# Sums of x blocks made two pairs ahead on buffers of their own, and squares of rows behind the copies of sums, in an attention and token-mixing kernel

## The chip, the cores and the metric

The kernel runs on one core of a Trainium2 chip. The metric is the time of one execution in microseconds (us) on the device; the figure before is the median of three runs. Five engines work side by side: TensorE (PE; its weight loads are PEld), VectorE (DVE), ScalarE (ACT), GpSimd (POOL) and SyncE (SP), which here only issues DMAs. POOL and ACT issue DMAs too.

## The reference

```python
x = A_x                                             # (1, 2048, 640) float32
g = sigmoid((x * gate_w).sum(-1, keepdims=True))
qkv = x @ wqkv                                      # 32 heads of 20
p = softmax(q @ k.T * 20 ** -0.5)                   # for each head
a = (p @ v) @ wo
h = layernorm(x)                                    # over the 640 channels
u = gelu(einsum("bsd,sf->bdf", h, w1) + b1)         # mixing over the 2048 tokens
b = einsum("bdf,fs->bds", u, w2) + b2
out = g * a + (1 - g) * b.transpose
```

Everything is float32.

## The kernel before

A product in full precision is made of three matmuls: each operand is split into a high part (rounded copy, on ScalarE) and a low part (the rest, a subtraction on VectorE), and the products high-high, high-low and low-high are summed in PSUM. `hi_lo` is this split.

The stages in order of time are: the products of x with the first two groups of columns of q and of k (`qk_unit(m, w, q)`: 128 columns m by 512 rows q, m below 5 for q, from 5 on for k); the product for v together with the sums for the gate and for the mean of each row; the rest of q and k, with the normalized rows h; the two products of the token mixing with the first scores beside them; attention; and the last product with wo.

Each `qk_unit` puts 15 matmuls into a PSUM bank, copies it out as a high part `evh` (ScalarE) and a low part `evl` (VectorE, a ring of two buffers) and stores both, to q_d or k_d. For the first three column groups of k (c = 0, 1, 2) it also forms the difference of two neighbouring 512-row blocks: `kf` keeps a copy of an even unit, the odd unit subtracts, splits the difference into `dh` and `kf` and stores four tiles to kd_d. For c = 1 (unit m = 6) kf and dh lie in the ring k8 (three buffers), and the four stores are issued by POOL.

The product for v is a fast 2 by 2 block scheme with seven products, for each pair of 128-row blocks of x. Eight pairs, `i` = 0 to 7, each with:

- `v_load(i)`: a DMA on SP brings the pair's block of x transposed, `vx`. `v_sums(i)`: POOL makes four sums of its quarters, T1 to T4, in `vr`. `v_split(i)`: `hi_lo` of vr into `vT`, in the ring k8. vx, vr and the rows `xn` lie in the ring q4, of six buffers.
- `split_wv` splits the eight combinations of v's weights (A11, A12, A22, S1 to S4, and number 7) among the eight qk units n = 0 to 7 ahead of this stage.
- `v_head(i)`: products X (A11) and Y (A12), 15 matmuls; the first copy of X's sum into `sn` on ScalarE (`v_snap`); the split of the next pair; an output tile.
- `v_body(i)`: X goes on with T2 S2 (6 matmuls), second copy of X; Z with T1 S1 (9); X goes on with T3 S3 (6), third copy of X; an output tile. T3's products add to the bank that the second copy reads.
- `v_tail(i)`, which runs after the head of pair i + 1: X with T4 A22, Z with S4, 18 matmuls, two output tiles, then `negm`, the negative mean of the rows, on VectorE, and `stats_unit` for both row blocks: the sum of squares of (x − mean) on ScalarE, from rows `xn` that POOL's DMA loads.

An output tile `vt` (a ring of three) gets its constant columns by memsets on POOL, its data from ScalarE (L536, where no sum is added) or VectorE (L538), and is stored to v_d by SP.

In this part the order of TensorE, ScalarE and VectorE is that of the program text (`manual_schedule`); the order of POOL and SP is chosen by the scheduler from its own estimate of times. Every queue works in order. A tile of a ring waits until the former tile in its buffer is no longer used. `xr` is a ring of two 640-column buffers, for weights of q and k before the split.

Of the kernel before, what the change touches and what calls it, by code (L numbers as in the profile page):

```python
# [7 lines left out]
F32 = mybir.dt.float32  # L8
F32R = mybir.dt.float32r
# [4 lines left out]
P = 128  # L14
S, D, H, DH, F = 2048, 640, 32, 20, 1728
NP = H // 2
NT = S // P
NC = D // P
# [13 lines left out]
def gated_mix(ctx, tc, xT, x, wqk, wv0, wv1, wo, w1, w1t, b1, w2, b2, out):  # L32
    nc = tc.nc
# [17 lines left out]
    def mm3(ps, pairs, between=lambda i: None):  # L51
        n = len(pairs)
        for i, (ah, al, bh, bl) in enumerate(pairs):
            for k, (a, b) in enumerate(((ah, bh), (ah, bl), (al, bh))):
                nc.tensor.matmul(ps, a, b, start=(i == 0 and k == 0), stop=(i == n - 1 and k == 2))  # L55
            between(i)
# [28 lines left out]
    def one_tile(shape, name):  # L85
        n = one_count[0] % 4
        one_count[0] += 1
        return psum.tile(shape, F32, tag=("s3", "pv", "one0", "one1")[n], bufs=1, name=name)
# [9 lines left out]
    def k8(shape, dt, name):  # L98
        return base.tile(shape, dt, tag="k8", bufs=3, name=name)

    def q4(shape, dt, name):
        return base.tile(shape, dt, tag="q4", bufs=6, name=name)
# [189 lines left out]
    p1 = p1s.enter_context(tc.tile_pool(name="p1", bufs=1, side="right"))  # L292
# [5 lines left out]
    def w_dma(m, eng=nc.scalar):  # L298
        raw = p1.tile([P, NC, P], F32, tag="xr", bufs=2, name=f"wr{m}")
        eng.dma_start(raw, wqk[m])  # L300
        return raw
# [9 lines left out]
    k_first = {}  # L311

    def qk_unit(m, w, q):
        wh, wl = w
        ps = one_tile([P, 512], f"qk{m}_{q}")
        mm3(ps, [(wh[:, c], wl[:, c], xh[c][q], xl[c][q]) for c in range(NC)], *([keep_warm] if m == q == 0 else []))
        hi = p1.tile([P, 512], F32R, tag="evh", bufs=3, name=f"evh{m}_{q}")
        tag, bufs = ("kf", 1) if (m, q) == (2 * NC - 1, 3) else ("evl", 2)
        lo = p1.tile([P, 512], F32R, tag=tag, bufs=bufs, name=f"evl{m}_{q}")
        hi_lo(hi, lo, ps, hi_eng=nc.scalar)  # L320
        c = m - NC
        dst = q_d if m < NC else k_d
        rows = slice((m % NC) * P, (m % NC + 1) * P)
        cols = slice(q * 512, (q + 1) * 512)
        stores = [(dst[i, rows, cols], t.bitcast(F32)) for i, t in enumerate((hi, lo))]
        if (m, q) == (2 * NC - 1, 3):
            return stores
        for a in stores:
            nc.sync.dma_start(*a)
        if not 0 <= c * P < DROWS:  # L330
            return
        if q % 2 == 0:
            if q == 0 or c == 2:
                k_first[c] = p1.tile([P, 512], F32, tag="kf", bufs=1, name=f"kf{c}_{q}")
            elif c:
                k_first[c] = k8([P, 512], F32, f"kf{c}_{q}")
            else:
                k_first[c] = px.tile([P, 512], F32, tag="kf2", bufs=1, name=f"kf{c}_{q}")
            nc.vector.tensor_copy(k_first[c], ps)
            return  # L340
        put = nc.gpsimd.dma_start if c < 2 else nc.sync.dma_start
        put(kd_d[0, rows, cols], hi.bitcast(F32))
        put(kd_d[1, rows, cols], lo.bitcast(F32))
        kd = k_first.pop(c)
        nc.vector.tensor_sub(kd, kd, ps)
        if c == 2:
            dh = p1.tile([P, 512], F32R, tag="evh", bufs=3, name=f"dh{c}_{q}")
        elif c:
            dh = k8([P, 512], F32R, f"dh{c}_{q}")
        else:  # L350
            dh = px.tile([P, 512], F32R, tag="dh", bufs=1, name=f"dh{c}_{q}")
        hi_lo(dh, kd.bitcast(F32R), kd, hi_eng=nc.scalar)
        cols = slice((q - 1) * 512, q * 512)
        put(kd_d[0, rows, cols], dh.bitcast(F32))
        put(kd_d[1, rows, cols], kd)
# [33 lines left out]
    xr = {(c, 0): x_dma(c, 0) for c in range(NC)}  # L389
    raws = {NC: w_dma(NC, nc.sync)}  # L390
# [27 lines left out]
    A11, A12, A22, S1, S2, S3, S4 = range(7)  # L418
# [4 lines left out]
    r11, r21, r22 = (wr[0][:, 2 * i: 2 * i + 2] for i in range(3))  # L423
    r12, rc = wr[1][:, :2], wr[1][:, 2:5]
# [6 lines left out]
    def split_wv(i, raw):  # L431
        hi_lo(wvh[i], wvl[i], raw, hi_eng=nc.scalar)
# [7 lines left out]
    def v_load(i):  # L440
        v_xs[i] = q4([P, 4, 2 * P], F32, f"vx{i}")
        nc.sync.dma_start(v_xs[i], xT[:4 * P, 2 * P * i: 2 * P * (i + 1)].rearrange("(c p) s -> p c s", p=P))

    def v_sums(i):
        r = v_xs.pop(i)
        r11, r12, r21, r22 = (r[:, 2 * k: 2 * k + 2, n * P:(n + 1) * P] for k in range(2) for n in range(2))
        v_rs[i] = q4([P, 8, P], F32, f"vr{i}")
        t = [v_rs[i][:, 2 * j: 2 * j + 2] for j in range(4)]
        nc.gpsimd.tensor_sub(t[T1], r12, r11)
        nc.gpsimd.tensor_sub(t[T2], r22, t[T1])  # L450
        nc.gpsimd.tensor_sub(t[T3], r22, r12)
        nc.gpsimd.tensor_sub(t[T4], r21, t[T2])

    def v_split(i):
        t = v_ts[i] = k8([P, 2, 8, P], F32R, f"vT{i}")
        hi_lo(t[:, 0], t[:, 1], v_rs.pop(i), hi_eng=nc.scalar)

    for n in range(8):
        if n == 1:
            split_wv(A11, r11)  # L460
            split_wv(A12, r12)
        if n == 2:
            split_wv(A22, r22)
            nc.vector.tensor_add(r22, r22, r21)
            nc.vector.tensor_sub(r21, r11, r21)
            v_load(0)
        if n == 3:
            split_wv(S1, r22)
            nc.vector.tensor_sub(r22, r22, r11)
            v_sums(0)  # L470
        if n == 4:
            nc.vector.tensor_sub(rc[:, 2:], rc[:, :1], rc[:, 1:2])
            split_wv(7, rc)
            v_load(1)
        if n == 5:
            split_wv(S2, r22)
            nc.vector.tensor_sub(r12, r12, r22)
        if n == 6:
            split_wv(S3, r21)
        if n == 7:  # L480
            split_wv(S4, r12)
        qk_unit((1, NC + 1)[n // 4], w[(1, NC + 1)[n // 4]], n % 4)
        if n == 0:
            w[NC + 1] = load_w(NC + 1, raws[NC + 1])
    v_split(0)
    nc.gpsimd.dma_start(b1_t, b1)
    nc.gpsimd.dma_start(b2_t, b2)
    xjs = {}

    def stats_load(t):  # L490
        if t < NT:
            xjs[t] = q4([P, D], F32, f"xn{t}")
            nc.gpsimd.dma_start(xjs[t], x[t * P:(t + 1) * P, :])

    def stats_unit(t):
# [13 lines left out]
    def v_w(i, k):  # L509
        return wvh[i][:, k], wvl[i][:, k]  # L510
# [34 lines left out]
    def v_head(i):  # L545
        t0 = 2 * i
        v_ps[i] = [v_bank(i, k) for k in range(3)]
        X, Y, Z = v_ps[i]
        v_mm(X, [(v_x(t0, k), v_w(A11, k)) for k in range(2)], True)
        v_mm(Y, [(v_x(t0, 2 + k), v_w(A12, k)) for k in range(2)] + [(v_x(t0, 4), v_w(7, 0))], True)  # L550
        a = v_snap(i, 0)
        if i + 1 < NT // 2:
            v_split(i + 1)
        v_out(0, t0, Y, a)

# [11 lines left out]
    def v_tail(i):  # L567
        t0, t1 = 2 * i, 2 * i + 1
        X, Y, Z = v_ps.pop(i)
        v_mm(X, [(v_t(i, T4, k), v_w(A22, k)) for k in range(2)] + [(v_x(t0, 4), v_w(7, 1))], False)  # L570
        v_mm(Z, [(v_x(t1, 2 + k), v_w(S4, k)) for k in range(2)] + [(v_x(t1, 4), v_w(7, 2))], False)
        v_ts.pop(i)
        v_out(1, t0, X)
        v_out(0, t1, Z, v_sn.pop(i))
        c = slice(t0, t0 + 2)
        nc.vector.tensor_scalar_mul(negm[:, c], gs[:, c, 1], -1.0 / D)
        for t in (t0, t1):
            stats_unit(t)

    for i in range(NT // 2):  # L580
        if i + 1 < NT // 2:
            v_sums(i + 1)
        if i + 2 < NT // 2:
            v_load(i + 2)
        v_head(i)
        if i:
            v_tail(i - 1)
        for t in (2 * i, 2 * i + 1):
            stats_load(t)
        v_body(i)  # L590
        if i == NT // 2 - 3:
            raws[2] = w_dma(2)
        if i == NT // 2 - 1:
            w[2] = load_w(2, raws[2])
    qk_unit(2, w[2], 0)
    v_tail(NT // 2 - 1)
    nc.scalar.activation(rstd, ssq, AF.Sqrt, bias=eps_t, scale=1.0 / D)
    nc.vector.reciprocal(rstd, rstd)
    nc.scalar.activation(g_t, gs[:, :, 0], AF.Exp, scale=-1.0)
# [340 lines left out]
    for n, _ in enumerate(steps):  # L940
# [5 lines left out]
        while done + 2 <= S_AHEAD and dve_work(done) < dve_room(n):  # L946
            if done == 48:
                s_src[1] = base_stack(1, False, None)
            if done == 4 * 128 + 40:
                held, drip[:] = list(drip), []  # L950
                st_src[0] = base_stack(0, True, None)
                put = lambda *a: drip.append(lambda: nc.sync.dma_start(*a))
# [253 lines left out]
    for p in range(NP):  # L1206
# [3 lines left out]
        for it in range(32):  # L1210
# [10 lines left out]
            if it == 14 and due_stack:  # L1221
                n = due_stack.pop()
                if n < NP:
                    s_src[n] = s_stack(n)
            if p == NP - 1:
# [4 lines left out]
                if it in (5, 20, 25):  # L1230
                    q = (5, 20, 25).index(it)
# [78 lines left out]
    for t in range(2, NT):  # L1310
        q = {4: 4, 7: 5, 10: 6, 12: 7}.get(t)
# [67 lines left out]
```

## Time and profile before

| | |
|---|---|
| median of three runs | 1792.18 us (1789.33 to 1794.43) |
| profiled execution | 1789.76 us |
| its span, from the first to the last record | 1787.9 us |
| mean granted TensorE clock | 0.994 |
| busy: PE | 1760.3 us (98%) |
| ACT | 1488.6 us (83%) |
| DVE | 1252.4 us (70%) |
| POOL | 690.7 us (39%) |

The profile comes from one execution. A row of a timeline gives the start in us from the span's start, the length, engine, line, operation, the tile written and those read, and in brackets how long the engine had been idle before and what released it. L502 is the matmul of the values' product, L525 the copy sn, L41 and L44 the high and low part of a split, L497 the squares, L342, L343, L354 and L355 the stores to kd_d. A list of waits gives the total, the number and the longest. "issue" is time in which an engine waited for nothing that the profile shows.

### The profile page before, as it was taken

The numbers are of one execution on the slowest core, as the hardware profiler recorded it, in microseconds if no ns is written. First come the engines' busy times: TensorE is split into PE (matmuls) and PEld (weight loads), VectorE is DVE, ScalarE is ACT, GpSimd is POOL, SyncE is SP. The second block draws the span as 40 slices with busy tenths as digits, with TensorE's granted clock in tenths as the row PEclk, the third lists the DMA queues.
The fourth block names the chain that finished last, engine by engine and source line by source line (L and its number), as shares of the span: only waits on it lengthen the run. The fifth ranks groups of instructions, "written<-read, shape, count | busy, mean of one in ns | idle before, by whom it ended". The sixth has DMA issues, their size and how long they took to land.

```text
span 1787.9 us, 39575 instructions
## 1 busy us (share of the span) xinstructions
PE 1760.3 (98%) x14972; PEld 1088.5 (61%) x14972; DVE 1252.4 (70%) x2443; ACT 1488.6 (83%) x2547; POOL 690.7 (39%) x1025
## 2 busy tenths in 40 slices
PE   9789999999999999999999999999999999999999
PEld 7688899999999999733333333333333333333379
DVE  5532369989899988877676767676777667677336
ACT  4344368888888888699999999999999999999951
POOL 1451658789878777412111211111231212111320
PEclk9899999999999999999999999999999999999999
DMA  9764986566677555336304314234173143311345
GB/s 329 225 206 155 293 241 171 153 177 184 184 190 184 152 154 157 99 74 141 73 19 95 65 32 92 50 70 103 35 144 76 26 102 76 79 20 43 125 158 181
DMA packets 160433, 229.39 MB, mean 128 GB/s; under 512 B 66684, under 2 KB 97292, under 8 KB 156816
## 3 DMA queue, kind: packets, MB, share of 16 engines
q1 hardware_dynamic: 141454, 197.01, 40.3%
q0 software_dynamic: 15568, 23.95, 5.6%
q10 hardware_dynamic: 3220, 5.90, 1.2%
q8 instruction: 118, 1.93, 0.5%
q14 instruction: 73, 0.60, 0.1%
HBM read 171.07 MB, written 55.36 MB: 127 GB/s over the span
## 4 chain that ended last, share of the span: by engine, by line
PE 93%; issue 2%; DMA 2%; ACT 1%; DVE 1%; POOL 1%; SPq 0%; DVEq 0%; ACTq 0%; POOLq 0%
PE pv L1058 28%; PE st L1157 22%; PE s L213 12%; PE y L49 10%; PE u L49 9%; PE qk L55 5%; PE v L502 2%; PE a L1277 1%; PE a_one L1277 1%; PE a_pv L1277 1%; PE a_s L1277 1%; ACT xn L497 0%; DMA v_d<-vt 0%; DMA kd_d<-dh 0%; DMA k_d<-evl 0%
## 5 line engine op out<-in xcount | busy, mean ns | idle before, releaser
L219 DVE TENSOR_REDUCE mx<-s 128x1 f32<-128x512 f32 x1280 | 834.7, 686 | 282.8 <-PE s L213 155.8
L1175 ACT ACTIVATE p<-st 128x512 f32<-128x512 f32 x1022 | 560.9, 614 | 0.0
L1058 PE MATMUL pv<-p,v 128*32 128x512 f32 x4088 | 544.5, 605 | 0.0
L1164 ACT ACTIVATE p<-st 128x1024 f32<-128x1024 f32 x511 | 529.8, 1037 | 1.2 <-PE st L1157 1.1
L1157 PEld LDWEIGHTS st<-qs_True,ks_True 62*128 62x128 f32 x2044 | 243.9, 185 | 432.6 <-ACT p L1164 426.8
L1157 PE MATMUL st<-qs_True,ks_True 62*128 62x512 f32 x2044 | 494.1, 445 | 0.0
L213 PE MATMUL s<-ks_False,qs_False 60*128 60x512 f32 x1152 | 323.2, 391 | 0.4 <-ACT p L1175 0.2
L44 POOL TENSOR_TENSOR wl<-wr,wh 128x512 fp32r<-128x512 f32 x228 | 275.3, 1218 | 61.4 <-ACT wh L41 46.7
L238 DVE CUSTOM_DVE_ANT_0 ov<-s,ov 128x512 f32<-128x512 f32 x384 | 263.7, 687 | 35.8 <-PE s L213 24.9
L213 PE MATMUL s<-sk,sq 60*128 60x512 f32 x896 | 281.3, 394 | 0.0
L228 ACT ACTIVATE ov<-s 128x512 f32<-128x512 f32 x384 | 228.4, 597 | 61.4 <-PE s L213 54.1
L1039 POOL DMA_DIRECT2D l_d<-oev x124 | 60.5, 494 | 382.1 <-DVE oev L1031 378.3
L49 PE MATMUL y<-gh,wh 64*128 64x320 f32 x896 | 198.0, 305 | 0.0
L213 PEld LDWEIGHTS s<-ks_False,qs_False 60*128 60x128 f32 x1152 | 194.2, 184 | 3.1 <-ACT p L1175 0.7
L1058 PEld LDWEIGHTS pv<-p,v 128*32 128x32 f32 x4088 | 80.5, 108 | 187.0 <-issue 175.3
L49 PE MATMUL y<-gh,wl 64*128 64x320 f32 x832 | 191.4, 305 | 0.0
L49 PE MATMUL y<-gl,wh 64*128 64x320 f32 x832 | 191.4, 305 | 0.0
L49 PE MATMUL u<-hh,wh 64*128 64x320 f32 x864 | 191.3, 304 | 0.0
L49 PE MATMUL u<-hl,wh 64*128 64x320 f32 x864 | 191.2, 304 | 0.0
L41 ACT ACTIVATE wh<-wr 128x512 fp32r<-128x512 f32 (+3 forms) x247 | 146.8, 598 | 41.6 <-PE y L49 15.6
L49 PE MATMUL u<-hh,wl 64*128 64x320 f32 x800 | 179.6, 304 | 0.0
L213 PEld LDWEIGHTS s<-sk,sq 60*128 60x128 f32 x896 | 166.2, 186 | 15.0
(217 smaller groups left out, 2478.0 us busy)
## 6 DMA issues: line engine op xcount, KB each, us to landing
wr<-in_w_dram SPq DMA_DIRECT2D x192, 256.0 KB
ks_True<-k_d SPq DMA_DIRECT2D x96, 160.0 KB
qs_True<-q_d SPq DMA_DIRECT2D x192, 80.0 KB
qs_False<-q_d SPq DMA_DIRECT2D x96, 80.0 KB
v_d<-vt SPq DMA_DIRECT2D x32, 212.0 KB
sk<-k_d SPq DMA_DIRECT2D x42, 160.0 KB
sq<-q_d SPq DMA_DIRECT2D x84, 80.0 KB
v<-v_d SPq DMA_DIRECT2D x15, 424.0 KB
```

Source lines behind the costliest of these rows:

```text
L41: nc.scalar.activation(hi, src, AF.Copy)
L44: (lo_eng or nc.vector).tensor_sub(lo, src, hi.bitcast(F32))
L49: nc.tensor.matmul(ps[k], a[r], b[r], start=start, stop=stop)
L55: nc.tensor.matmul(ps, a, b, start=(i == 0 and k == 0), stop=(i == n - 1 and k == 2))
L213: nc.tensor.matmul(ps, qs[half][r, t * P:(t + 1) * P], ks[r, kc * 512:(kc + 1) * 512], start=True, stop=True)
L219: nc.vector.tensor_reduce(mx[:, slot, j, t: t + 1], ps, axis=AX.X, op=OP.max)
L228: nc.scalar.activation(over[j, kc], ps, AF.Relu)
L238: nc.vector.tensor_tensor_reduce(ov, ps, ov, 1.0, -3.0e38, OP.add, OP.max, mx[:, slot, j, t: t + 1])
L1058: nc.tensor.matmul(pv[r: r + 32, :], v_tiles[p][:, kt, VW * j: VW * j + 32], pt[j, c], start=(kt == 0), stop=(kt == NT - 1))
L1157: nc.tensor.matmul(ps, ks[r, kt * P:(kt + 1) * P], qs[qh][r, c * 512:(c + 1) * 512], start=True, stop=True)
L1164: nc.scalar.activation(pt, ps, AF.Exp, scale=SCALE)
L1175: nc.scalar.activation(pt, ps, AF.Exp, scale=SCALE)
```

## The change

The sums of a block are made two pairs ahead of their use and the loads three ahead, and the split of the second pair is made before the loop. The rows xn leave q4 for the ring xr; kf and dh of c = 1 leave k8 for xr, and their stores to kd_d go from POOL's queue to SP's. The splits of v's weights move to earlier units. The squares of a pair stand behind the third copy of the next pair's body, and the rows of the next squares are loaded after them. The weights of the next q unit (m = 2) are loaded into q4 and split one pair earlier.

```diff
             elif c:
-                k_first[c] = k8([P, 512], F32, f"kf{c}_{q}")
+                k_first[c] = p1.tile([P, 512], F32, tag="xr", bufs=2, name=f"kf{c}_{q}")
...
-        put = nc.gpsimd.dma_start if c < 2 else nc.sync.dma_start
+        put = nc.gpsimd.dma_start if c < 1 else nc.sync.dma_start
...
         elif c:
-            dh = k8([P, 512], F32R, f"dh{c}_{q}")
+            dh = p1.tile([P, 512], F32R, tag="xr", bufs=2, name=f"dh{c}_{q}")
...
         if n == 1:
             split_wv(A11, r11)
             split_wv(A12, r12)
+            v_load(0)
         if n == 2:
             split_wv(A22, r22)
             nc.vector.tensor_add(r22, r22, r21)
             nc.vector.tensor_sub(r21, r11, r21)
-            v_load(0)
+            v_sums(0)
         if n == 3:
             split_wv(S1, r22)
             nc.vector.tensor_sub(r22, r22, r11)
-            v_sums(0)
-        if n == 4:
             nc.vector.tensor_sub(rc[:, 2:], rc[:, :1], rc[:, 1:2])
             split_wv(7, rc)
+        if n == 4:
+            split_wv(S2, r22)
+            nc.vector.tensor_sub(r12, r12, r22)
             v_load(1)
         if n == 5:
-            split_wv(S2, r22)
-            nc.vector.tensor_sub(r12, r12, r22)
+            split_wv(S3, r21)
+            split_wv(S4, r12)
+            v_sums(1)
         if n == 6:
-            split_wv(S3, r21)
-        if n == 7:
-            split_wv(S4, r12)
+            v_split(0)
+            v_load(2)
         qk_unit((1, NC + 1)[n // 4], w[(1, NC + 1)[n // 4]], n % 4)
...
-    v_split(0)
+    v_split(1)
...
     def stats_load(t):
         if t < NT:
-            xjs[t] = q4([P, D], F32, f"xn{t}")
+            xjs[t] = p1.tile([P, D], F32, tag="xr", bufs=2, name=f"xn{t}")
...
-        if i + 1 < NT // 2:
+        if 1 < i + 1 < NT // 2:
             v_split(i + 1)
...
         nc.vector.tensor_scalar_mul(negm[:, c], gs[:, c, 1], -1.0 / D)
-        for t in (t0, t1):
+    def v_stats(i):
+        for t in (2 * i, 2 * i + 1):
             stats_unit(t)
 
+    for i in range(2):
+        stats_load(i)
     for i in range(NT // 2):
-        if i + 1 < NT // 2:
-            v_sums(i + 1)
         if i + 2 < NT // 2:
-            v_load(i + 2)
+            v_sums(i + 2)
+        if i + 3 < NT // 2:
+            v_load(i + 3)
         v_head(i)
         if i:
             v_tail(i - 1)
-        for t in (2 * i, 2 * i + 1):
-            stats_load(t)
         v_body(i)
-        if i == NT // 2 - 3:
-            raws[2] = w_dma(2)
-        if i == NT // 2 - 1:
+        if i:
+            v_stats(i - 1)
+            for t in (2 * i, 2 * i + 1):
+                stats_load(t)
+        if i == NT // 2 - 4:
+            raws[2] = q4([P, NC, P], F32, "wr2")
+            nc.scalar.dma_start(raws[2], wqk[2])
+        if i == NT // 2 - 2:
             w[2] = load_w(2, raws[2])
     qk_unit(2, w[2], 0)
     v_tail(NT // 2 - 1)
+    v_stats(NT // 2 - 1)
```

## The prediction

> **What bounds the kernel now.** I read the page first, then the table of windows by stage, the list of waits of TensorE, the timelines of TensorE, ScalarE and VectorE around the waits, and the list of DMA issues.
>
> The table of windows, whose columns are stretch and length, then busy time and count of PE, PEld, DVE, ACT, POOL, then granted clock, DMA share and GB/s:
>
> ```profile
> 62.50:161.60 99.10, 77.09 (x450) 72.46 (x449) 33.63 (x89) 38.08 (x84) 38.30 (x137) 0.90 0.58 190
> 161.60:1787.90 1626.30, 1622.18 (x14270) 966.83 (x14268) 1179.71 (x2298) 1422.35 (x2415) 635.86 (x853) 1.00 0.45 118
> ```
>
> TensorE is the bound. From 161.6 us to the end it idles 4.1 of 1626 us, at the full clock. Ahead of that lies the stage of the values' product, which the change rewrites: 77.1 of 99.1 us busy, at a mean clock of 0.90. Since TensorE has no slack behind it, what this stage gains or loses moves the end by as much. Who holds TensorE there, in the list of waits (total, times, longest):
>
> ```profile
> PE v L502 <- ACT sn L525: 20.1, 9, 9.4
> PE qk L55 <- ACT wh L41: 1.2, 1, 1.2
> PE v L502 <- DVE vT L44: 0.5, 1, 0.5
> ```
>
> ScalarE's copy of a sum (sn) ends nine of the waits. In TensorE's timeline (start, length, ... , idle before and who ended it) the first three of the nine:
>
> ```profile
> 74.93 0.64 PE L502 MATMUL v<-wvh,vT 128*128 128x322 f32 x1 [9.39 <-ACT sn L525]
> ...
> 81.53 0.42 PE L502 MATMUL v<-wvh,vT 128*128 128x322 f32 x1 [2.00 <-ACT sn L525]
> ...
> 92.15 0.42 PE L502 MATMUL v<-wvh,vT 128*128 128x322 f32 x1 [0.80 <-ACT sn L525]
> ```
>
> The 9.39 and the 2.00 us stand before the first and the second pair of rows; the other seven (20.1 − 9.4 − 2.0 = 8.7 us) come once in each pair from the second on, like the 0.80 us at 92.15, always in front of the third product T3 with S3.
>
> **What stands before sn.** ScalarE's timeline, at the start and in one steady pair:
>
> ```profile
> 72.97 0.63 ACT L41 ACTIVATE dh<-kf 128x512 fp32r<-128x512 f32 x1 [6.25 <-DVE kf L345]
> 73.51 1.04 ACT L41 ACTIVATE vT<-vr 128x1024 fp32r<-128x1024 f32 x1
> 74.46 0.42 ACT L525 ACTIVATE sn<-v 128x322 f32<-128x322 f32 x1
> 80.09 1.06 ACT L41 ACTIVATE vT<-vr 128x1024 fp32r<-128x1024 f32 x1 [5.21 <-DMA kd_d<-dh]
> ...
> 99.98 0.81 ACT L497 ACTIVATE xn<-xn,negm 128x640 f32<-128x640 f32 x1
> 100.70 0.19 ACT L497 ACTIVATION_READ_ACCUMULATOR xn<-xn,negm 128x1 f32 x1
> 100.79 0.42 ACT L525 ACTIVATE sn<-v 128x322 f32<-128x322 f32 x1
> ```
>
> There are three causes, one for each part of the change. The first sn (74.46) is queued behind the last dh, which waited for VectorE. The second sn runs right after the split vT at 80.09, which waited 5.2 us for a store of dh: vT takes its buffer from the ring k8, where dh and kf lay. In the steady pairs two squares (L497) are in front of sn.
>
> **The steps and their cost.** No instruction is added or removed; order, buffers and queues change. For the floor I need the pace of the matmuls:
>
> ```profile
> 86.20:91.10 4.90, 4.90 (x35) 4.89 (x33) 2.52 (x8) 1.57 (x5) 3.04 (x7) 1.00 0.24 88
> 74.90:92.10 17.20, 13.94 (x69) 13.02 (x69) 6.21 (x16) 5.77 (x12) 6.69 (x16) 0.79 0.59 177
> 92.10:151.15 59.05, 51.12 (x324) 49.56 (x324) 18.07 (x59) 25.38 (x59) 24.09 (x109) 0.97 0.59 200
> 151.15:161.60 10.45, 9.19 (x40) 7.58 (x41) 2.07 (x4) 2.17 (x5) 0.00 (x0) 0.84 0.17 63
> 74.90:78.60 3.70, 3.19 (x10) 2.79 (x11) 1.36 (x2) 0.00 (x0) 2.84 (x5) 0.50 0.94 231
> ```
>
> In the first row TensorE is full and its clock too: 33 weight loads, one for each matmul, in 4.90 us, 0.148 us a step (its matmul count also holds those in flight at both edges). From 92.1 to 151.15 a pair of row blocks is 54 matmuls (324 in six pairs), so 8.0 us at this pace.
>
> (a) **The first wait.** VectorE's timeline; the store that I hold responsible; the landing times of all stores to kd_d, issued by POOL; a store by SP, in the chain of work that ended last; and the list of DMA issues, in which the last figure is the median landing time:
>
> ```profile
> 62.56 0.68 DVE L44 TENSOR_TENSOR evl<-qk,evh 128x512 fp32r<-128x512 f32 x1
> ...
> 67.11 0.82 DVE L44 TENSOR_TENSOR wvl<-wvr,wvh 128x644 fp32r<-128x644 f32 x1
> 71.61 0.69 DVE L44 TENSOR_TENSOR evl<-qk,evh 128x512 fp32r<-128x512 f32 x1 [3.68 <-issue]
> ```
> ```profile
> 65.45 0.54 POOL L343 DMA_DIRECT2D kd_d<-evl  x1
> ```
> ```profile
> DMA to landing us min/median/max: 2.7/5.4/8.0
> ```
> ```profile
> 17.67 5.38 DMA k_d<-evl
> ```
> ```profile
> xn<-in_x_dram POOLq DMA_DIRECT2D x16, 320.0 KB, 4.3
> ...
> kd_d<-evl POOLq DMA_DIRECT2D x2, 256.0 KB, 6.3
> ```
>
> The last evl has a ring of two; its buffer is free when the store of two units earlier has landed, 65.45 + 6.3 = 71.7. From its start to the start of TensorE it is 74.93 − 71.61 = 3.3 us (evl, kf, dh, one vT, sn). The edit moves these four stores of each second unit from POOL's queue, where they stood behind the sums of a block, to SP. On the other side the splits S3 and S4 (0.82 us each on VectorE, as at 67.11, overlapping a little) now come ahead of the earlier evl. It ran from 62.56 to 63.24 and its store sat on POOL until 65.45; now it ends at about 64.7, and the store leaves SP at 64.8 to 65.2. The split vT of the first pair moves ahead of the last evl, into VectorE's 3.68 us of idle time; the second pair's vT takes its place ahead of sn, so the 3.3 us stay. With 5.4 us (the store by SP) the store lands at 70.2 to 70.6, with 6.3 at 71.1 to 71.5, and TensorE starts at 73.5 to 74.8. I take −1.0 us, between. The ends, with the extremes of 2.7 and 8.0 us, are −2.7 (then VectorE's own queue is last: 67.11 + 0.82 and some 1.1 of vT give 69) and +1.6.
>
> The Trainium skill (DMA: Bandwidth & Descriptors, Issuing engines are not separate DMA queues) says that another issuing engine saves only the time to issue, not the transfer; by it the landing stays 6.3 us, and this term is −0.1 to −0.5 instead of −1.0; no row here has one store on both queues.
>
> (b) **To the T3 of the second pair.** From 74.9 to 92.1 there are 69 matmuls, 10.2 us at 0.148, in 17.2 us. Excess 7.0: waits of 0.5 + 2.0 + 0.8 = 3.3, slow clock 3.7. All three waits go: the first vT is ready, the second is split before the loop on buffers that no store holds, the squares are behind. Of the clock, the ten matmuls after the first wait stay slow (3.2 us of busy time instead of 1.5): 1.7 stay. Gain −5.3. What is next late there: nothing on ScalarE, since sn of the second pair has then only two sn ahead of it.
>
> (c) **Six pairs**, 92.1 to 151.15: 59.05 − 324 × 0.148 = 11.0 us of excess, 7.9 waits and 3.1 clock. The squares now come after the third sn of a pair and before the first of the next, which TensorE needs only 27 matmuls (4.0 us) after it could be made; they take 1.75 us. So they hide: −11.0. Lower bound in (e).
>
> (d) **The end**, 151.15 to 161.6: 24 matmuls of v (3.55) and 15 of qk, at 3.45 in all by the chain's next piece, make 7.0 of 10.4. The weights of qk are now split a pair earlier, and the squares are away: −3.4. The load of these weights stays on ScalarE's queue, one pair earlier.
>
> ```profile
> 161.61 3.45 PE qk L55 x15
> ```
>
> (e) **What takes the place.** At 8.0 us a pair four vt are stored from three buffers, so a buffer must come round in 6 us. Rows of ScalarE's timeline, of POOL's waits and of the chain show where that ring already bites, and how long a store takes:
>
> ```profile
> 106.33 0.51 ACT L536 ACTIVATE vt<-v 128x160 f32<-128x160 f32 x2 [1.59 <-DMA v_d<-vt]
> ```
> ```profile
> POOL vt L530 <- DMA v_d<-vt: 35.4, 18, 5.4
> ```
> ```profile
> 103.66 3.18 DMA v_d<-vt
> ```
>
> L536 is ahead of the second sn on ScalarE. At this pace its product is done 24 matmuls into the pair (3.55 us) and T3 needs that sn at the 48th (7.1); less L536 and sn themselves (0.51 and 0.42) 2.6 us are to spare. The charge lies between 0 (the slack covers it) and the whole 1.6 us in six pairs, 10 us. I take 0.7 a pair, nearer to zero because of the slack: +4.2.
>
> (f) **Moves at no charge.** vx and vr keep the six q4 buffers to themselves, so SP's load of vx no longer waits for one in front of stores of v_d. The eight stores taken from POOL free 8 × 0.54 us there and cost SP eight issues while it is otherwise waiting for evh and evl. xn has two buffers: POOL's issue of the next two waits for the squares, with the memsets of vt and the sums of blocks queued behind; those sums are made two pairs ahead, which covers it. If that cover fails, it is rival 3.
>
> Sum: −1.0 − 5.3 − 11.0 − 3.4 + 4.2 = −16.5 us. The profiled execution took 1789.76 us (span 1787.9), 2.4 below the median of 1792.18. So 1773.3 for one like it, and 1775.7 beside the median.
>
> **The clock** carries 3.7 + 3.1 + 2.2 − 1.7 = 7.3 us of this (2.2: the 3.4 of the end less its wait of 1.2). The windows with the granted clock as the third figure from the end:
>
> ```profile
> 80.00:85.00 5.00, 3.47 (x14) 3.47 (x15) 2.31 (x6) 2.06 (x4) 0.54 (x1) 0.70 0.54 182
> 95.00:100.00 5.00, 5.00 (x36) 5.00 (x35) 2.55 (x8) 2.03 (x6) 2.80 (x10) 1.00 0.71 251
> ```
>
> After the idle time of 2.00 us that ended at 81.53 the clock was 0.70; after the 0.80 at 92.15 it stayed at 1.00. So waits shorter than the first also cost clock, from somewhere between 0.8 and 2.0 us, and where they go the clock comes back. The Trainium skill (TensorE: Matmul & The Clock Gate, Why this matters for your kernels) lets the clock fall only after idle times over about 3 us; by that rule the later slow stretches are not the waits' doing and may stay; the row after the 2.00 us speaks against it (rival 4).
>
> **Rivals.** For the third, one of the four sums of a block on POOL (minimum, median, maximum in ns):
>
> ```profile
> L449 POOL TENSOR_TENSOR vr<-vx x8: 728/734/1282, 48.9 to 127.4; 128x256 f32<-128x256 f32 x8
> ```
>
> 1. The vt ring becomes the bound of the loop: the full 10 us of (e). For it: three buffers, 18 memsets that waited for a store. Against: a store takes 3.2 us where the chain shows one, and a round in 6 us has room for that, the fill and the memset. Gain 10.7, 1781.5 us.
> 2. Only the squares pay: the first sn comes no earlier, or later, and the wait of the second vT moves ahead of it. For it: dh and its store still stand in the same chain, on another ring of two. Against: vT's buffers no longer hold dh. Term (a) and half of (b) go: gain 16.5 − 1.0 − 2.7 = 12.8; with the 1.6 of (a) added, 11.2. That is 1779 to 1781 us.
> 3. The other side: the loop of xn. Squares free a buffer, POOL issues the load, it lands, the next squares start; with two buffers this is a closed loop of 1.85 (both squares and the step to POOL) + hold on POOL + 4.3 landing − 0.8 (the squares overlap). At no hold it is 5.4 us, under the 8.0. Squares late on ScalarE make sn of the next pair late. Before, six pairs took 59.05/6 = 9.84 us each. Terms (a), (b), (d) bring 9.7, so for a loss beyond 0.3% (5.4) a pair must exceed 9.84 + 15.1/6 = 12.4, a hold of 7.0 us: the longest wait of a memset on POOL (5.4) and a little over two of the sums (0.74 each). With the 5.4 and all four sums (2.9) it is 13.6 us a pair: 22.6 − 9.7 = 13 us slower, 1805. With the 5.4 alone, 10.8 a pair, it is 4 us faster: no measurable change.
> 4. The clock stays: gain 16.5 − 7.3 = 9.2, 1783 us.
>
> **How the numbers follow.** Forecast 0.60; rival 1 0.17; rival 2 0.07; rival 4 0.04; rival 3 0.12, half of it slower and half within the bound. Within 0.3% (5.4 us, about what a measurement of this kernel can tell from no change) 0.06, slower 0.06, faster 0.88. The range goes from 1769 (no charge for the ring, and the best of (a)) to 1786 (rivals 1 and 4 in part together); it leaves out rival 3 and some extremes.
>
> **What would show it.** TensorE's list of waits on sn should fall from 20.1 us to about 10, nearly all in the first wait, with its end near 73 to 75 us; T3 should have hardly any wait; the stage should end near 145 us; the granted clock should be 1.00 from about 80 us on. A wait of sn behind L497, or of L497 for xn, would show rival 3; a wait of L536 for v_d rival 1. The forecast would be wrong if the order that the scheduler gives POOL and SP, which the change doesn't write out, puts the loads of xn behind memsets that wait for stores.

## The result, and the profile after

| | before | after |
|---|---|---|
| median | 1791.97 us (1789.33 to 1794.43) | 1769.2 us (1768.6 to 1770.04) |
| profiled execution | 1789.76 us | 1769.21 us |
| its span | 1787.9 us | 1767.3 us |
| mean granted clock | 0.994 | 0.997 |

The ratio is 0.9873, with a 95% interval of 0.9856 to 0.9891: 22.8 us faster by the medians of four runs each, 20.6 us by the spans. The forecast of 16.5 us, 1775.7 us, was too careful: the measured time stands 0.2 us inside the low end of the range, 1769.0.

The windows of the kernel after: the stage to the end of the values' product, all that follows it, and the stage from the first body on (columns as in the table of before).

```profile
62.50:140.22 77.72, 70.12 (x449) 69.00 (x448) 33.55 (x88) 36.34 (x82) 35.99 (x128) 0.93 0.77 249
140.22:1767.30 1627.08, 1622.72 (x14269) 966.97 (x14268) 1180.31 (x2298) 1422.91 (x2415) 636.31 (x853) 1.00 0.45 118
72.66:140.22 67.56, 67.56 (x433) 66.94 (x434) 25.35 (x77) 31.89 (x75) 31.50 (x123) 0.97 0.74 241
```

The first row, with the same 450 or so matmuls, was 99.10 us before and is 77.72 now, 21.4 us less. The rest of the kernel took 1627.1 us instead of 1626.3: the gain lies in this stage alone, and 0.8 us of it are given back later. The third row is what is worth remembering: from the first product that needs a sum to the end of the stage, TensorE is busy for 67.56 of 67.56 us. The chain of work that ended last says the same in three pieces without a break:

```profile
72.66 61.45 PE v L504 x399
134.10 3.43 PE qk L55 x15
137.54 2.68 PE v L504 x18
```

TensorE's list of waits from 62.5 to 141 us, whole, and the two rows of its timeline behind it:

```profile
PE v L504 <- ACT sn L527: 5.8, 1, 5.8
PE v L504 <- DVE kf L345: 1.8, 1, 1.8
```
```profile
65.31 0.39 PE L504 MATMUL v<-wvh,xh 128*128 128x322 f32 x1 [1.81 <-DVE kf L345]
...
72.66 0.64 PE L504 MATMUL v<-wvh,vT 128*128 128x322 f32 x1 [5.78 <-ACT sn L527]
```

Nine waits on sn, 20.1 us, have become one of 5.78 us; it ends 2.27 us earlier than before (74.93). ScalarE's timeline shows why. At the start the copy sn is still behind dh and a split, but nothing waits for a store; in a later pair the squares (now L499) stand behind the third copy and are over before the next one is needed, with the split behind that:

```profile
70.70 0.63 ACT L41 ACTIVATE dh<-kf 128x512 fp32r<-128x512 f32 x1 [2.95 <-DVE kf L345]
71.24 1.04 ACT L41 ACTIVATE vT<-vr 128x1024 fp32r<-128x1024 f32 x1
72.19 0.42 ACT L527 ACTIVATE sn<-v 128x322 f32<-128x322 f32 x1
...
86.02 0.44 ACT L527 ACTIVATE sn<-v 128x322 f32<-128x322 f32 x1 [1.78 <-PE v L504]
86.36 0.83 ACT L499 ACTIVATE xn<-xn,negm 128x640 f32<-128x640 f32 x1
...
87.98 0.42 ACT L527 ACTIVATE sn<-v 128x322 f32<-128x322 f32 x1
88.31 1.05 ACT L41 ACTIVATE vT<-vr 128x1024 fp32r<-128x1024 f32 x1
```

The clock comes back within 8 us of the one wait that is left, and stays:

```profile
72.60:76.60 4.00, 3.94 (x15) 3.94 (x16) 1.47 (x4) 0.45 (x2) 2.46 (x4) 0.50 1.10 375
76.60:80.60 4.00, 4.00 (x27) 4.00 (x27) 0.81 (x3) 1.83 (x3) 1.55 (x4) 0.94 0.98 287
...
90.10:138.20 48.10, 48.10 (x318) 47.48 (x317) 18.83 (x60) 24.38 (x58) 19.42 (x92) 1.00 0.64 208
```

### The profile page after: what moved, and what is told of

It is laid out like the page before. It is cut to its first block, busy times and chain, and to the rows that moved or that the text cites. A ratio compares the mean times of both kernels' runs of the same rounds, so it can differ in the third digit from the quotient of the medians.

```text
span 1767.3 us, 39559 instructions
## 1 busy us (share of the span) xinstructions
PE 1753.6 (99%) x14972; PEld 1085.1 (61%) x14972; DVE 1253.2 (71%) x2443; ACT 1489.0 (84%) x2547; POOL 690.2 (39%) x1017
## 4 chain that ended last, share of the span: by engine, by line
PE 96%; issue 1%; DVE 1%; DMA 1%; ACT 1%; POOL 0%; ACTq 0%; DVEq 0%; POOLq 0%
PE pv L1067 29%; PE st L1166 22%; PE s L213 12%; PE y L49 10%; PE u L49 10%; PE qk L55 5%; PE v L504 4%; PE a L1286 1%; PE a_one L1286 1%; PE a_pv L1286 1%; PE a_s L1286 1%; DMA k_d<-evl 0%; PE a L49 0%; DVE wvl L44 0%; DMA kd_d<-kf 0%
## 5 line engine op out<-in xcount | busy, mean ns | idle before, releaser
L44 POOL TENSOR_TENSOR wl<-wr,wh 128x512 fp32r<-128x512 f32 x228 | 275.3, 1218 | 63.1 <-ACT wh L41 48.1
```

The source lines that it names most:

```text
L44: (lo_eng or nc.vector).tensor_sub(lo, src, hi.bitcast(F32))
```

## The experiments

Theory: three independent causes held TensorE, one for each part of the change (the squares in front of sn; the stores that stood on POOL's queue, and through them the ring k8; the split and the sums that came too late), and each part pays by taking one away. The rivals: the squares are all of it, the ring of vt charges for the faster pace, or idle time costs clock by another rule than the prediction's. Each experiment's time is set against runs of the kernel before on the same chip (medians of 1791.75, 1793.2, 1793.81 and 1792.1 us in the four groups) and, less sharply, against the 1769.2 of after.

### The squares alone, on the kernel before

```diff
-        for t in (t0, t1):
+
+    def v_stats(i):
+        for t in (2 * i, 2 * i + 1):
             stats_unit(t)
 
+    for i in range(2):
+        stats_load(i)
...
-        for t in (2 * i, 2 * i + 1):
-            stats_load(t)
         v_body(i)
+        if i:
+            v_stats(i - 1)
+            for t in (2 * i, 2 * i + 1):
+                stats_load(t)
...
+    v_stats(NT // 2 - 1)
```

> The kernel before with one part of the change: the squares behind the third copy of the next pair's body, their rows loaded after them (still in q4). Theory (the squares in front of sn make the wait of T3): all waits of T3 go, also the 0.8 us of the second pair; the first two waits (9.4 and 2.0 us) and the wait for the weights of qk stay. 1792 - 11 - 0.8 - about 1.5 = 1779 us, 1777 to 1782. Rival (the pairs were long because SP's loads of vx stood in front of the stores of v_d and the vt ring was late): the pairs stay near 9.5 us and the time at 1787 to 1791.

1781.99 us, ratio 0.9948 (0.9932 to 0.9965): 9.8 us gained, as the theory has it. TensorE's list of waits in the stage:

```profile
PE v L502 <- ACT sn L525: 11.1, 4, 6.5
PE qk L55 <- ACT wh L41: 2.8, 1, 2.8
```

From nine waits to four: five of the seven waits of T3 are gone. Two of T3 remain, because ScalarE's output tile waits for a store of v_d, as rival 1 of the prediction has it. TensorE's row, ScalarE's, and SP's row in the list of waits:

```profile
115.09 0.42 PE L502 MATMUL v<-wvh,vT 128*128 128x322 f32 x1 [0.84 <-ACT sn L525]
```
```profile
114.21 0.50 ACT L536 ACTIVATE vt<-v 128x160 f32<-128x160 f32 x2 [3.65 <-DMA v_d<-vt]
```
```profile
SPq L442 <- POOL vt L532: 8.6, 3, 3.1
```

Here SP's load of vx (L442) waits for POOL, with the next stores of v_d queued behind it. The kernel after has no such wait of SP, and no such wait of ScalarE.

Not all of the 9.8 us is the squares' own. The theory let the first two waits stay at 9.4 and 2.0 us; they became 6.54 and 2.65, and the first body starts 1.97 us earlier. TensorE's row, and the store of evl in the chain of work that ended last:

```profile
72.96 0.64 PE L502 MATMUL v<-wvh,vT 128*128 128x322 f32 x1 [6.54 <-ACT sn L525]
```
```profile
64.41 3.66 DMA kd_d<-evl
```

The stores to kd_d are still on POOL's queue here, but the first two loads of xn now leave POOL at 52.35 and 53.99, well ahead of them, and not at 64.34 and 67.04, among them. The store landed 3.7 us after 64.41, and the last evl (69.65) did not wait for it.

### The change without the squares' part

```diff
         nc.vector.tensor_scalar_mul(negm[:, c], gs[:, c, 1], -1.0 / D)
+        v_stats(i)
+
...
         if i:
-            v_stats(i - 1)
...
-    v_stats(NT // 2 - 1)
```

> The changed kernel with the squares back in the tail, in front of the second copy of sums; everything else as changed. Theory: T3 waits 0.8 to 1 us in each pair again, and the clock falls in some: 7 x 0.9 = 6 us of waits and up to 5 of clock, 1775 to 1780 us. Rival (sums and loads ahead are what shortens the pairs): 1770 to 1772 us.

1780.18 us, ratio 0.9936 (0.9919 to 0.9952), 11.0 us above the kernel after. Its list of waits, the first and the last of the six waits of T3 that are nearly alike, and the one longer wait ahead of them:

```profile
PE v L504 <- ACT sn L527: 13.0, 8, 5.6
```
```profile
87.86 0.42 PE L504 MATMUL v<-wvh,vT 128*128 128x322 f32 x1 [2.06 <-ACT sn L527]
...
98.56 0.42 PE L504 MATMUL v<-wvh,vT 128*128 128x322 f32 x1 [0.90 <-ACT sn L527]
...
144.39 0.42 PE L504 MATMUL v<-wvh,vT 128*128 128x322 f32 x1 [0.89 <-ACT sn L527]
```

The six pairs from the T3 of the second to that of the last take 144.39 − 87.86 = 56.5 us here; the same six took 59.05 us before, 51.6 with the squares alone, and take 48.1 after. So of the 11 us that they lost, putting the squares back returns 8.4, and the squares alone bring 7.5: some 8 belong to the squares and 3 to the rest. The two halves add up: the squares alone bring 9.8, all but the squares 11.6, together 21.4 of the 22.8.

### The four stores of c = 1 back on POOL

```diff
-        put = nc.gpsimd.dma_start if c < 1 else nc.sync.dma_start
+        put = nc.gpsimd.dma_start if c < 2 else nc.sync.dma_start
```

> The changed kernel with the eight stores of c = 1 back on POOL's queue. Theory: the store of evl leaves later, behind the sums on POOL, lands 1 to 2 us later and takes the first wait of TensorE from 5.8 to 7 or 8 us: 1770 to 1771.5 us. Rival (which queue issues does not matter, VectorE's own order sets the first sn): 1769.2, no change.

1775.97 us, ratio 0.9913 (0.9898 to 0.9928): 6.8 us above after, three times the most that was expected. The path, from POOL's timeline to VectorE's, ScalarE's and TensorE's:

```profile
67.27 0.54 POOL L343 DMA_DIRECT2D kd_d<-evl  x1
```
```profile
74.29 0.69 DVE L44 TENSOR_TENSOR evl<-qk,evh 128x512 fp32r<-128x512 f32 x1 [4.36 <-DMA kd_d<-evl]
```
```profile
76.77 0.63 ACT L41 ACTIVATE dh<-kf 128x512 fp32r<-128x512 f32 x1 [8.33 <-DMA kd_d<-dh]
```
```profile
78.72 0.63 PE L504 MATMUL v<-wvh,vT 128*128 128x322 f32 x1 [10.71 <-ACT sn L527]
```

POOL issues the store at 67.27, behind its sums, and the last evl gets the buffer at 74.29, 7.0 us later. In the kernel after SP issues the same store at 64.97, and the last evl, in VectorE's timeline, starts at 69.35 without a wait:

```profile
64.97 0.42 SPq L343 DMA_DIRECT2D kd_d<-evl  x1
```
```profile
69.35 0.67 DVE L44 TENSOR_TENSOR evl<-qk,evh 128x512 fp32r<-128x512 f32 x1
```

So the store by SP is over in less than 4.4 us. Of the 4.9 us between the two starts of evl, 2.3 are the later issue and at least 2.6 a longer time to landing. Then dh waits for its own ring (xr): the store of the dh before it was late too.

That POOL's queue itself makes the landing longer is not shown. The same store, issued by POOL, landed in 3.7 us in the kernel with the squares alone, and a store by SP takes 7.4 us in the next experiment. Here SP issues a load of vx (512 KB) at 66.77, just ahead of the store; in the kernel after, SP's loads of vx leave at 58.23 and 69.27. Whether that load, or other traffic, made the store slow was not separated.

### kf and dh of c = 1 back in the ring k8

```diff
-                k_first[c] = p1.tile([P, 512], F32, tag="xr", bufs=2, name=f"kf{c}_{q}")
+                k_first[c] = k8([P, 512], F32, f"kf{c}_{q}")
...
-            dh = p1.tile([P, 512], F32R, tag="xr", bufs=2, name=f"dh{c}_{q}")
+            dh = k8([P, 512], F32R, f"dh{c}_{q}")
```

> The changed kernel with kf and dh of c = 1 back in the ring k8. Theory: the split vT of the second pair takes its buffer from the store of kf or dh again, and since it now stands in front of the first sn, TensorE starts the first body at 77 to 80 instead of 72.7: 1774 to 1778 us. Rival (the stores on SP land early enough that the ring does not matter): 1769 to 1770 us.

1779.76 us, ratio 0.9936 (0.9921 to 0.995), 10.6 us above after and more than expected. ScalarE's split, the store in front of it in the chain of work that ended last (issued by SP), and TensorE's first wait:

```profile
81.06 1.06 ACT L41 ACTIVATE vT<-vr 128x1024 fp32r<-128x1024 f32 x1 [8.48 <-DMA kd_d<-dh]
```
```profile
73.55 7.41 DMA kd_d<-dh
```
```profile
82.50 0.64 PE L504 MATMUL v<-wvh,vT 128*128 128x322 f32 x1 [13.46 <-ACT sn L527]
```

The split made ahead of the loop must now wait for the store of the last dh, and it stands in front of the first sn: buffers apart from k8 are not only a help to the early split, it is harmful without them.

### The second split back in the first head

```diff
-    v_split(1)
...
-        if 1 < i + 1 < NT // 2:
+        if i + 1 < NT // 2:
             v_split(i + 1)
```

> The changed kernel with the split vT of the second pair back in the first head, behind the first sn. Theory (the second wait came from the buffer in k8, not from the place of the split): the first sn comes 0.9 us earlier and no second wait returns: 1768 to 1768.5 us. Rival (the split ahead of the loop removed the second wait): the first wait shorter by 0.9 us, and a second one of 1 to 2 us with its clock: 1770 to 1772 us.

1773.2 us, ratio 0.9888 (0.987 to 0.9906), 4.0 us above after; the interval overlaps that of after, but each of the four runs (from 1771.26 us up) is above each of after's. Neither expectation met it. The theory's mechanism held all the same: TensorE has one wait on sn, of 4.6 us, so the first wait is 1.1 us shorter and no second one returned. The loss came later in the loop, in two waits of TensorE for VectorE's tiles (3.6 us). The longer one, in TensorE's timeline:

```profile
109.01 0.41 PE L503 MATMUL v<-wvh,xh 128*128 128x322 f32 x1 [2.65 <-DVE vt L539]
```

The lists of waits name the squares and the output tiles:

```profile
ACT xn L498 <- DMA xn<-in_x_dram: 3.9, 4, 1.7
DVE vt L539 <- DMA v_d<-vt: 16.5, 6, 6.4
```

The chain of work that ended last names what the tile ahead of this wait (VectorE, 108.40) waited for, a store of an earlier tile:

```profile
101.83 6.38 DMA v_d<-vt
```

The sn that this tile needs was ready at 103.3, so the late squares did not hold it: the ring of vt did, rival 1's mechanism, with its three buffers. POOL's order, which the scheduler chose anew for this text, has loads of xn behind sums and ahead of memsets of vt, and two of these issues (1.09 us) stand further back in the same chain. The same kernel with the loads of xn issued by ScalarE was to tell whether the hold of the loads on POOL is the cause:

```diff
-            nc.gpsimd.dma_start(xjs[t], x[t * P:(t + 1) * P, :])
+            nc.scalar.dma_start(xjs[t], x[t * P:(t + 1) * P, :])
```

> The kernel with the second split back in the first head, and the loads of xn issued by ScalarE instead of POOL. There the squares waited for xn (0.4 to 1.7 us, four times), whose loads stood behind sums on POOL, and TensorE twice for VectorE's tiles (3.6 us). Theory (the hold of the loads on POOL, in the order that the scheduler chose, cost the 4 us, not the place of the split): 1768.5 to 1770.5 us, no wait of TensorE behind the first. Rival (the late second split pushes VectorE's tiles back, whoever issues the loads): 1772 to 1774 us.

1777.44 us, ratio 0.9919 (0.9905 to 0.9933), slower still, for a reason that was not foreseen. ScalarE's timeline, and the chain behind it:

```profile
80.92 0.44 ACT L526 ACTIVATE sn<-v 128x322 f32<-128x322 f32 x1 [8.66 <-DMA kd_d<-kf]
```
```profile
81.42 61.86 PE v L503 x399
```

The first two loads stand on ScalarE's queue in front of the first sn, and their buffer (xr) is held by the store of kf: the first sn comes 8.7 us late. Behind it there is no wait in 399 matmuls, where the kernel with POOL's loads had its waits. That fits a part of POOL's loads in the loss but does not show it, since everything behind the first sn comes 8.7 us later here.

### One buffer fewer for the output tiles

```diff
-        vt = pvp.tile([P, 8, NPAIR], F32, tag="vt", bufs=3, name=f"vt{half}_{t}")
+        vt = pvp.tile([P, 8, NPAIR], F32, tag="vt", bufs=2, name=f"vt{half}_{t}")
```

> The changed kernel with two buffers for vt instead of three. Four output tiles in 8.0 us then leave 4 us for fill, store (3.2 us or more) and memset. Theory (the ring of three has slack for TensorE, 4.2 us of charge were too many): with two it binds, ScalarE waits with its tile ahead of the second sn, 2 to 4 us a pair: 1782 to 1800 us. Rival (waits for vt fall on VectorE and POOL alone and never reach TensorE): 1769 to 1772 us.

1771.31 us, ratio 0.9881 (0.9867 to 0.9896): 2.1 us above after, where the theory of a tight ring asked for 13 and more. Its waits:

```profile
PE v L504 <- ACT sn L527: 7.0, 2, 5.6
```
```profile
DVE vt L540 <- DMA v_d<-vt: 13.0, 6, 5.1
```
```profile
ACT vt L538 <- DMA v_d<-vt: 5.4, 3, 2.1
```

18.4 us of waits for the stores of v_d reach TensorE as one wait of 1.4 us (7.0 − 5.6). So the theory that two buffers bind fell. Nor did the rival hold to the letter, by which no such wait reaches TensorE. In the order of the kernel after, the third buffer is worth 2 us at most.

### How long a wait costs clock

The second copy of a sum is repeated, so that T3 waits for it by a set time, in three pairs only (four, six and nine copies; in a second kernel three, five and seven):

```diff
         b = v_snap(i, 1)
+        for _ in range({2: 4, 4: 6, 6: 9}.get(i, 0)):
+            nc.scalar.activation(b, X, AF.Copy)
```

> The changed kernel with the second copy of the sum repeated on ScalarE, 4, 6 and 9 times more in the pairs 2, 4 and 6, so that T3 waits once in each. At 0.34 to 0.42 us a copy less some 0.65 us of slack, idle times of about 0.9, 1.6 and 2.8 us, 5.3 in all. Theory (idle times from somewhere between 0.8 and 2.0 us cost clock): slow stretches after the second and the third, 1.7 to 3 us each: 1778 us, 1776 to 1780. Rival (the clock falls only after idle times over about 3 us, as the Trainium skill has it, TensorE: Matmul & The Clock Gate): only the idle time itself: 1774 to 1775 us, clock 1.00 in all windows.

> As the run before it with 3, 5 and 7 more copies: idle times of about 0.5, 1.2 and 2.0 us, 3.7 in all. Theory: no clock lost after the first, after the 1.2 us perhaps, after the 2.0 us 1.7 to 3 us. Rival: no clock lost anywhere, 1773 us.

1778.22 us, ratio 0.992 (0.9905 to 0.9935), and 1777.18 in the one run of the second. The windows of 4 us that begin at the end of the idle time, of the first kernel, after waits of 1.15, 2.04 and 3.45 us (6.6 in all):

```profile
95.00:99.00 4.00, 3.89 (x26) 3.89 (x27) 0.56 (x2) 2.01 (x5) 0.71 (x7) 1.00 0.75 265
113.40:117.40 4.00, 3.99 (x27) 3.99 (x28) 0.56 (x2) 2.79 (x7) 1.23 (x5) 1.00 0.35 105
133.10:137.10 4.00, 3.96 (x17) 3.96 (x18) 0.56 (x2) 1.95 (x5) 0.41 (x1) 0.60 0.00 0
```

Of the second, after 1.57 and 2.51 us (0.68 left the clock at 1.00 too):

```profile
113.50:117.50 4.00, 3.92 (x26) 3.92 (x27) 0.55 (x2) 2.75 (x8) 1.18 (x6) 1.00 0.33 99
132.30:136.30 4.00, 3.91 (x19) 3.92 (x20) 0.56 (x2) 2.75 (x8) 1.42 (x8) 0.71 0.15 56
```

And of the kernel with the squares put back, after its wait of 2.06 us:

```profile
87.80:91.80 4.00, 3.94 (x16) 3.94 (x17) 0.56 (x2) 1.16 (x4) 3.52 (x14) 0.58 0.87 286
```

The first kernel's time met the theory partly by luck: the idle times were longer than the 5.3 us expected, and one of them cost clock, not two.

The clock was kept after 2.04 us and lost after 2.06, and after the 2.00 of the kernel before. In these kernels waits of up to 1.57 us cost none, 2.51 and 3.45 did. The length of one wait does not decide alone. With kf and dh in k8 the granted clock was 0.50 from 67.0 us on, soon after a wait of 1.76 us that ended at 66.56; at the end of this stage in the kernel before, two waits close together (0.85 us to 151.20 and 1.21 us to 153.57) were followed by 0.57 in 4 us; and the first of the better versions below kept 1.00 after 2.74 us. What else decides is not shown. A loss costs about ten matmuls of 27 in 4 us, 1.5 us.

### Better versions

The first wait of 5.78 us is left. Three versions put the head of the first pair between the copies of the last qk unit and its difference, so that the first sn runs ahead of dh; the splits of S4 and of the second pair follow the unit:

```diff
-    def qk_unit(m, w, q):
+    def qk_unit(m, w, q, between=lambda: None):
...
+        between()
         kd = k_first.pop(c)
...
+    qk_unit(NC + 1, w[NC + 1], 3, lambda: v_head(0))
+    v_split(1)
+    split_wv(S4, r12)
```

> The changed kernel with the first head put between the copies and the difference of the last qk unit before it, so that the first sn is made ahead of the last dh and ahead of the second vT on ScalarE; the split S4 moves behind them too. Theory (the first wait is ScalarE's order alone: dh waits for VectorE, and sn behind it): the first sn comes at about 68 us, TensorE starts the first body at 68 to 69 instead of 72.7, and with an idle time under 3 us instead of 5.8 part of the slow clock goes as well: 1763 to 1766 us. Rival (VectorE's queue is the bound there, and what moves behind comes back as a later wait for its bank or for vT): 1767 to 1770 us.

1768.04 us (1766.37 to 1769.6), ratio 0.9859 (0.9844 to 0.9874), which overlaps that of after: no clear gain, as the rival has it. TensorE's timeline, and the window behind its second row:

```profile
69.22 0.42 PE L504 MATMUL v<-wvh,vT 128*128 128x322 f32 x1 [1.25 <-ACT sn L527]
...
74.71 0.42 PE L504 MATMUL v<-wvh,vT 128*128 128x322 f32 x1 [2.74 <-ACT sn L527]
```
```profile
74.71:90.10 15.39, 14.73 (x97) 14.47 (x98) 4.89 (x14) 5.98 (x13) 11.69 (x31) 1.00 0.99 323
```

The first body starts 3.4 us earlier, and 15 matmuls later 2.74 of them are lost again, since the second sn now has dh, the split of the second pair and that of S4 in front of it. The mean clock of this profile is 1.000, and yet its stage ends at 140.23, where that of after ends: most of the wait was moved, not removed.

The second version has the loads of xn on ScalarE as well, and fell into the same trap as above: its first wait is 1.08 us, but the second sn stands behind loads whose buffer the store of kf holds, and TensorE waits 8.39 us for it:

> The kernel with the first sn early, and the loads of xn issued by ScalarE. Theory: as with the first sn early alone, or up to 1 us less, since no hold of a load on POOL can reach TensorE: 1762 to 1766 us. Rival (two issues of 0.34 us a pair on ScalarE delay sn): 1 to 3 us more.

1775.22 us, ratio 0.99 (0.9887 to 0.9914), 7.2 us above the first version and more than the rival's 3. The third makes the first body early too, and leaves the first two loads on POOL:

```diff
-    def qk_unit(m, w, q):
+    def qk_unit(m, w, q, between=lambda: None, late=lambda: None):
...
         nc.vector.tensor_sub(kd, kd, ps)
+        late()
...
+    qk_unit(NC + 1, w[NC + 1], 3, lambda: v_head(0), lambda: v_body(0))
...
+            (nc.gpsimd if t < 2 else nc.scalar).dma_start(xjs[t], x[t * P:(t + 1) * P, :])
```

> The kernel with the first head put early, and the first body with it: both stand ahead of the last dh and of the split of the second pair; the loads of xn, the first two apart, are issued by ScalarE. Theory (what is left are ScalarE's places behind dh, 2.7 us in the second product of the first pair, and behind late xn, 1.2 us): both go, 1763 to 1766 us. Rival (VectorE's queue at this place is full, and the difference, its split and the second vT come late for the second pair instead): 1767 to 1770 us.

1771.56 us, ratio 0.989 (0.9873 to 0.9906), above both expectations. Its first pair runs as intended (68.00, after a wait of 1.24 us), but ScalarE's squares wait for the first rows, and TensorE for the sn behind them:

```profile
88.28 0.83 ACT L500 ACTIVATE xn<-xn,negm 128x640 f32<-128x640 f32 x1 [7.06 <-DMA xn<-in_x_dram]
```
```profile
91.18 0.64 PE L505 MATMUL v<-wvh,vT 128*128 128x322 f32 x1 [4.17 <-ACT sn L528]
```

POOL issues these first two loads only at 82.67, behind eight sums and the memsets of two tiles, from 74.03 on, and they land 5.4 and 6.1 us later. This is rival 3's mechanism, a hold on POOL that makes the squares late and sn behind them. A version with these loads at a better place was not tried. None of the three clearly beats the kernel after.

## Why the prediction was right, and where not

The three causes were the right ones. The squares are shown from both sides (9.8 us gained alone, 11.0 lost when put back), the buffers in k8 by +10.6 us and the stores' queue by +6.8 when undone. These three losses sum to 28 and not to 22.8, because the last two make the same first wait late. Not shown is that the early place of the second split pays: put back, it brought no second wait, and its +4.0 us came from the ring of vt. The sums and loads made further ahead, the moved splits of v's weights and the earlier weights of m = 2 were never undone by themselves, so what each of them brings is open.

One reading in the prediction was off, without changing its sum: the wait of 2.00 us stands before T3 of the first pair, 15 matmuls behind the first wait, and not before the second pair.

(a) **The first wait** was undersized: −1.0 was taken, −2.27 measured, within its ends. (Four other profiles of kernels with the same text ahead of the first body start it at 73.00 to 73.51 us, by which it is −1.4 to −1.9.) The term assumed that a store by SP lands in 5.4 to 6.3 us. It took less than 4.4, so that the last evl didn't wait for it at all: VectorE's own queue is last, the case that the term had as its lower end. What now holds the first sn is dh's wait for VectorE's difference kf and the split behind dh. That SP issues is not needed for this, since the squares alone, with the stores on POOL, moved the first body by 1.97 us. The Trainium skill (DMA: Bandwidth & Descriptors, Issuing engines are not separate DMA queues), by which only the issue time is saved, gave −0.1 to −0.5. More was measured, but the runs do not refute the rule: the same store by POOL took 3.7 us in one kernel and about 7 in another, so that the landing time changed without a change of queue.

(b), (c), (d) were right: −5.3, −11.0 and −3.4 were forecast, −4.9 (17.22 to 12.28 us), −10.9 (59.05 to 48.12) and −3.3 (10.41 to 7.16) measured. From the start of the first body to the end of the stage it took 161.61 − 74.93 = 86.7 us, and takes 67.6 now: −19.1. The slow rest after the first wait, put at 1.7 us, came out at about 2 (105 matmuls in the 17.5 us from 72.6 on, against 15.5 at 0.148).

(e) **The ring of vt** is the term that was mis-sized most: +4.2 was charged and 0 measured, as the 399 matmuls without a break show. VectorE still waited for stores of v_d, 10.1 us in three waits, but none of it reached TensorE. ScalarE, whose wait of 1.59 us was the ground for the term, has no such wait now. One thing that left with it is the load of vx that held SP's stores back (8.8 us in three waits before, 8.6 with the squares alone, none after), which point (f) had as a move "at no charge". That this is the cause is not shown: with the second split back in the first head SP has no such wait either, and there ScalarE waits four times for a store of v_d (5.4 us) and TensorE loses 3.6 us to the ring. So the 0 belongs to the order that POOL and SP have in this kernel, not to three buffers as such.

(f) held: no wait for xn reached TensorE. But the cover is thin, and it hangs on the order that the scheduler gives POOL: in the third of the better versions late loads of xn cost TensorE 4.17 us.

**The clock** came back as forecast, and rival 4 fell. The sentence behind it, that waits cost clock from somewhere between 0.8 and 2.0 us, holds with its upper part: the waits of 1.15 and 1.57 us that were set for it cost none. The Trainium skill's limit of about 3 us (TensorE: Matmul & The Clock Gate, Why this matters for your kernels) is too wide for these runs: the clock fell after 2.06 and 2.51 us, though it stood after 2.74 in one.

**To the median.** The profile before was 2.4 us below the median then known and this was added to the forecast; the profile after equals its median (1769.21 and 1769.2). One execution's distance is no constant to carry over. That the time fell inside the range, by 0.2 us, is partly luck: the low end stands for no charge for the ring and the best of (a), and nearly that came. The terms against the profiles: −16.5 forecast, −20.6 measured; of the 4.1 too few, 4.2 are (e), 1.3 are (a), less 0.6 of (b) to (d) and the 0.8 of the later stages.

## What to carry to other kernels

When an engine is late with a small piece that the bound engine needs (here a copy of 0.42 us), read what stands in front of it on its own queue, and put the work that nobody is waiting for behind it. Give early work buffers that no store still holds, for an early step on a held buffer stops all that is queued behind it, DMA issues with a buffer of their own to wait for included. And do not charge a ring for waits on an engine with slack: charge it for what the bound engine was seen to wait, and look again when the order of the queues changes.

## What was not expected of the hardware

- The time that a store of 256 KB takes to land does not go by the queue that issues it: the same store of evl on POOL's queue took 3.7 us with the squares alone and about 7 with the stores put back on POOL, and on SP's queue a store of evl took under 4.4 us in the kernel after and one of dh 7.4 with kf and dh in k8.
- The granted clock outlasted the waits of up to 1.57 us that were set for it without a trace, and about 2 us can go either way (2.04 kept it, 2.00 and 2.06 did not). Length alone does not decide: one wait of 2.74 us kept it and one of 1.76 did not.
- A queue with a DMA issue in it is held by that DMA's buffer: ScalarE did nothing for 8.66 us in front of a copy of 0.44 us.
